# Bounding the weights of a two-layer kernel: products of upper halves on TensorE in place of sums of absolute values on ScalarE

## The chip, the cores and the metric

One core of a Trainium2 chip runs the whole program. The metric is the device time of one execution in microseconds; the median of the runs is compared. Engines are named as the profile names them: PE is TensorE, DVE VectorE, ACT ScalarE, POOL GpSimd, and SP the queue that issues the transfers.

## The reference

Attention over pooled keys and values, then a two-layer block with a softmax-weighted linear unit and a layer norm. Inputs of the attention are float32, the weights `w_in` (512 x 1024), `w_out` (1024 x 512) and the gain come in as 64-bit numbers.

```python
# attention: B, H, S, D = 8, 8, 576, 64; keys and values pooled by 8
k_p = k.reshape(B, H, Sp, pool, D).mean(axis=3)
v_p = v.reshape(B, H, Sp, pool, D).mean(axis=3)
scores = scale * np.matmul(q, k_p.transpose(0, 1, 3, 2))
attn = softmax(scores)                      # over the 72 pooled keys
attn_out = np.matmul(attn, v_p)
# block: x is 4608 x 512
h = x @ w_in                                # 4608 x 1024
e = np.exp(h - h.max(-1)); sm = e / e.sum(-1)
solu = h * sm
ln = (solu - mean) / np.sqrt(var + 1e-06) * g_ln
return (ln @ w_out).astype(np.float32)      # 4608 x 512
```

## The kernel before

The 4608 rows of x are worked off in 36 tiles of 128. Per tile, `scores` (16 small matmuls), a softmax on DVE and ACT (`s_max`, `s_sub`, `s_exp`, `e_sum`, `e_rec`, `e_mul`, split by `e_hi` and `e_lo` into two f16 parts, turned by a DMA transpose `e_T`), `av` (16 matmuls of 128 columns into the PSUM tile xp), `x_hi` and `x_lo` (xT in two f16 parts), `mm1` (24 matmuls of 512 columns into hp, in three parts), `h_max` to `z_var` on DVE, ACT and POOL, two transposes `z_T`, `mm2` (24 matmuls into op) and the store. Everything that TensorE multiplies is split into a high and a low f16 part, so that three passes give nearly float32.

Before tile 0 the two weights must be brought into such pairs. Each weight is loaded as 64-bit words in four chunks of 128 partitions x 1024. For a chunk `w_exp` (ACT, the prelude that puts the upper word into float32 shape, into a tile u), `w_shift` (DVE), `w_tail` (DVE, which puts the lower bits in) make float32 of it. In between `w_abs` (ACT) sums the absolute values along the row into a column of bnd. `w_rmax` (DVE) takes the maximum over the four columns, `w_par` (PE, a matmul that spreads it over partitions), `w_all` (DVE) and `wi_scale` or `wo_scale` (DVE, small instructions ending in sw or sg) turn it into a power of two as scale. Then `w_hi` (ACT) writes the high part, and the low part comes for wi from `w_res` on PE (two pairs of a float32 matmul and a "minus" matmul into a PSUM tile res of tag h) and `w_lo` on ACT, for wo from `w_lo` on DVE. Tile 0 uses all high parts first (part 0 of `mm1` and `mm2`), the low parts last (part 2).

Each engine works in the order in which its instructions are issued. That order is a table, ORDER, of numbers of operations: a planner outside the kernel made it, and `op` only records each operation with its dependencies. Tags of buffers matter in three places: the scores use a single PSUM tile (tag s), which `e_mul` frees; hp and res share two (tag h); op has one (tag o). The names in the rows: u_wi and u_wo are the words after `w_exp`, wo and wir (for wi) and wor (for wo) hold the raw words, amx_q and amx_v the maxima of q and v, qm is the q of a mixed tile, vr and v the parts of the pooled v.

Of the kernel before, what the change touches and what calls it, by code (L numbers as in the profile page):

```python
# [9 lines left out]
BF16 = mybir.dt.bfloat16  # L10
# [150 lines left out]
def kernel(  # L161
# [363 lines left out]
    def w_shift(nm, c):  # L525
# [3 lines left out]
        )  # L529


    def w_abs(nm, c):
        st = wst[nm]
        if "bnd" not in st:
            st["bnd"] = const.tile([P, 4], F32, name=f"bnd_{nm}")
# [898 lines left out]
```

## Time and profile before

| | us |
|---|---|
| median of 3 runs | 481.98 |
| lowest and highest | 481.43, 486.75 |
| the profiled execution | 480.16 |
| its span on the core | 478.3 |
| PE busy in it | 443.8 (93%) |
| DVE, ACT, POOL busy | 357.6, 349.5, 334.4 |

The span is what the instructions of the core take from the first to the last; the execution's own time is 1.9 us longer. The granted clock is 1.00 (of 2.4 GHz) over the whole span. A row of the order of time gives a start, a length, the engine, the line, the tile written and read, and in brackets how long the engine had been idle before it and what it waited for.

### The profile page before, as it was taken

How to read it: one execution, taken by the hardware profiler on the slowest of the kernel's cores; microseconds unless marked ns; L12 is line 12 of the kernel's file. 1: busy time of each engine (PE TensorE's matmuls, PEld its weight loads, DVE VectorE, ACT ScalarE, POOL GpSimd, SP SyncE). 2: the span in 40 equal slices, each digit the busy share in tenths (PEclk: the TensorE clock that was granted, in tenths of full speed). 3: DMA queues.
4: the chain of work that ended last, by engine and by line, in shares of the span. 5: the costliest groups of instructions: out<-in, count | busy, mean ns of one | idle time of the engine just before them, and what ended most of it. 6: DMA issues, size and time to landing. Idle time of an engine off the chain costs nothing.

```text
span 478.3 us, 9037 instructions
## 1 busy us (share of the span) xinstructions
PE 443.8 (93%) x3100; PEld 230.5 (48%) x3100; DVE 357.6 (75%) x865; ACT 349.5 (73%) x578; POOL 334.4 (70%) x466
## 2 busy tenths in 40 slices
PE   0177999999999999999999999999999999999996
PEld 0033544555454555555545554555555554554462
DVE  4989999589777976778667986887776989674520
ACT  1889999859877588766976788668866589567751
POOL 7145889768999678995897659985987448526440
PEclk9999999999999999999999999999999999999999
DMA  8999795899899879989878779887999387656341
GB/s 275 413 372 176 203 156 106 208 230 213 176 242 178 214 165 201 213 206 214 201 176 163 184 188 201 215 191 173 212 210 195 61 188 119 103 113 144 80 119 58
DMA packets 201389, 89.14 MB, mean 186 GB/s; under 512 B 177664, under 2 KB 186112, under 8 KB 200832
## 3 DMA queue, kind: packets, MB, share of 16 engines
q1 hardware_dynamic: 201344, 88.57, 80.1%
q8 instruction: 24, 0.39, 0.4%
q14 instruction: 21, 0.17, 0.1%
HBM read 36.70 MB, written 9.44 MB: 96 GB/s over the span
## 4 chain that ended last, share of the span: by engine, by line
PE 74%; DVE 8%; DMA 6%; ACT 4%; POOL 4%; issue 2%; SPq 0%; POOLq 0%; ACTq 0%; DVEq 0%
PE op L1008 33%; PE hp L876 32%; PE xp L844 6%; DMA qT<-q 3%; PE sc L754 3%; POOL z L943 1%; DMA qr<-in_q_dram 1%; ACT wo L651 1%; DMA zT<-z 1%; DVE amx_q L349 1%; DMA eT<-e 1%; DVE z L921 1%; DVE e L794 1%; DVE sc L779 1%; DVE mx L765 1%
## 5 line engine op out<-in xcount | busy, mean ns | idle before, releaser
L876 PE MATMUL hp<-wi,xT 128*128 128x512 f16 x864 | 196.2, 379 | 3.2 <-ACT xT L852 3.2
L1008 PE MATMUL op<-wo,zT 128*128 128x512 f16 (+1 forms) x888 | 197.3, 373 | 1.0 <-ACT osb L1016 0.6
L876 PEld LDWEIGHTS <-xT 128*128 128x128 f16 x864 | 82.6, 98 | 97.8 <-ACT xT L852 4.0
L1008 PEld LDWEIGHTS <-zT 128*128 128x128 f16 x888 | 84.7, 98 | 91.7 <-issue 1.0
L943 POOL TENSOR_TENSOR z<-z,z 128x512 f16<-128x512 f32 x71 | 82.0, 1170 | 37.9 <-ACT z L930 35.5
L886 DVE TENSOR_REDUCE m<-hp 128x1 f32<-128x1024 f32 x36 | 44.0, 1222 | 30.5 <-PE hp L876 30.2
L823 POOL TENSOR_TENSOR e<-e,e 128x512 f16<-128x512 f32 x36 | 42.0, 1166 | 21.6 <-ACT e L816 21.6
L330 POOL TENSOR_TENSOR vr<-vr 128x512 f32<-128x512 f32 (+3 forms) x48 | 48.6, 1015 | 12.1 <-DMA vr<-in_v_dram 11.6
L897 ACT ACTIVATE z<-hp,nb,Hb 128x1024 f32<-128x1024 f32 x32 | 38.4, 1199 | 23.7 <-DVE nb L889 20.1
L935 ACT ACTIVATE z<-z,sz 128x1024 f16<-128x1024 f32 x36 | 41.2, 1144 | 17.0 <-DVE z L921 17.0
L921 DVE SCALAR_TENSOR_TENSOR z<-hp,rs,z 128x1024 f32<-128x1024 f32 x36 | 46.1, 1280 | 3.2 <-ACT z L897 1.6
L330 POOL TENSOR_TENSOR kr<-kr 128x512 f32<-128x512 f32 (+3 forms) x48 | 41.8, 878 | 2.8 <-DMA kr<-in_k_dram 2.3
L765 DVE TENSOR_REDUCE mx<-sc 128x8 f32<-128x576 f32 x36 | 27.2, 754 | 21.0 <-PE sc L754 20.9
L930 ACT ACTIVATE z<-z,sz 128x1024 f32<-128x1024 f32 x36 | 41.2, 1145 | 0.7
L844 PEld LDWEIGHTS <-vb 128*128 128x128 f16 x640 | 35.3, 98 | 8.9 <-issue 0.8
L1016 ACT ACTIVATE osb<-op,f 128x512 f32<-128x512 f32 (+1 forms) x37 | 24.7, 668 | 18.9 <-PE op L1008 10.8
L844 PE MATMUL xp<-eT,vb 128*128 128x128 f16 (+1 forms) x640 | 38.2, 214 | 0.1
L956 ACT ACTIVATE junk<-z 128x1024 f16<-128x1024 f32 x36 | 37.7, 1047 | 0.4
L735 POOL TENSOR_TENSOR q<-qr,q 128x512 f16<-128x512 f32 x28 | 32.6, 1169 | 4.7 <-ACT q L725 4.7
L779 DVE TENSOR_REDUCE sc<-sc 128x8 f32<-128x576 f32 x36 | 27.4, 760 | 11.4 <-ACT sc L775 11.4
L852 ACT ACTIVATE xT<-xp 128x512 f16<-128x512 f32 x36 | 21.3, 592 | 17.5 <-PE xp L844 17.3
L856 DVE SCALAR_TENSOR_TENSOR xT<-xp,xT 128x512 f16<-128x512 f32 x36 | 24.6, 682 | 6.7 <-ACT xT L852 6.7
(230 smaller groups left out, 585.3 us busy)
## 6 DMA issues: line engine op xcount, KB each, us to landing
kr<-in_k_dram SPq DMA_DIRECT2D x16, 512.0 KB, 4.3
qr<-in_q_dram SPq DMA_DIRECT2D x16, 512.0 KB, 4.9
vr<-in_v_dram SPq DMA_DIRECT2D x16, 512.0 KB, 4.6
out_dram<-osb SPq DMA_DIRECT2D x31, 256.0 KB, 2.8
wor<-in_moe_w_out_dram SPq DMA_DIRECT2D x4, 1024.0 KB, 8.9
wo<-in_moe_w_in_dram SPq DMA_DIRECT2D x2, 1024.0 KB, 6.7
wir<-in_moe_w_in_dram SPq DMA_DIRECT2D x2, 1024.0 KB, 10.7
out_dram<-osb SPq DMA_DIRECT2D x10, 128.0 KB, 2.3
```

What stands on the lines that cost most here:

```text
L330: nc.gpsimd.tensor_tensor(out=dst, in0=src[:, :, :n], in1=src[:, :, n : 2 * n], op=ALU.add)
L823: nc.gpsimd.tensor_tensor(out=m[:, 1], in0=e_pair(i)[:, :, :P], in1=m[:, 0], op=ALU.subtract)
L844: nc.tensor.matmul(xp[:, c, lo:hi], lhsT=vb[b % 2][:, x, c].rearrange("p j d -> p (j d)"), rhs=eT[:, e, lo:hi], start=(n == 0), stop=(n == 3),
L876: nc.tensor.matmul(hp[:, f], lhsT=xT[:, xt, c], rhs=wi[:, wt, c, f * 512 : (f + 1) * 512], start=(part == 0 and n == 0), stop=(part == 2 a ...
L886: nc.vector.tensor_reduce(out=small(i, "m"), in_=tl[i]["hp"], axis=AX.XY, op=ALU.max)
L897: nc.scalar.activation(z, t["hp"], AF.Exp, bias=t["nb"], scale=hsc(i, 0), accum_out=small(i, "se"))
L921: nc.vector.scalar_tensor_tensor(out=t["z"], in0=t["hp"], scalar=t["rs"], in1=t["z"], op0=ALU.mult, op1=ALU.mult, accum_out=small(i, "sz"),)
L930: nc.scalar.activation(t["zf"], t["zf"], AF.Identity, bias=t["sz"], scale=-float(DFF))
L935: nc.scalar.activation(t["z16"][:, 0], t["zf"], AF.Identity, bias=t["sz"], scale=-float(DFF))
L943: eng.tensor_tensor(out=t["z16"][:, 1, fs], in0=t["zf"][:, fs], in1=t["z16"][:, 0, fs], op=ALU.subtract)
L956: nc.scalar.activation(junk, t["zf"], AF.Square, scale=DFF**-0.5, accum_out=small(i, "V"))
L1008: nc.tensor.matmul(op_, lhsT=zT[:, zt, c], rhs=wo[:, wt, c, cols(hf)], start=(part == 0 and n == 0), stop=(part == 2 and n == len(todo) - 1),)
```

## The change

`w_abs` is replaced by `w_gram`: the upper 16 bits of each shifted word are read as bfloat16 (every second 16-bit word of u), and each block of 128 columns is multiplied with itself on PE, all 8 blocks of the 4 chunks of a weight summed into one 128 x 128 PSUM tile of tag o. Its diagonal holds sums of squares, and `w_rmax` takes the maximum of it per partition. `w_bound` halves the exponent instead of only masking it. The operations are recorded for PE instead of ACT, `w_rmax` reads the PSUM tile, and ORDER is new throughout. The diff without most of ORDER:

```diff
-    2, 1, 0, 3, 4, 12, 11, 56, 5, 6, 57, 53, 54, 7, 58, 50, 55, 8, 180, 51, 52, 13, 181, 65, 9, 75,
...
+    2206, 2208, 2207, 2262, 2263, 2209, 2210, 2162, 2211, 2212, 2163, 2164, 2165, 2166,
 )
...
-    def w_abs(nm, c):
+    def w_gram(nm, c):
         st = wst[nm]
-        if "bnd" not in st:
-            st["bnd"] = const.tile([P, 4], F32, name=f"bnd_{nm}")
-        g = p1.tile([P, DFF], BF16, tag="junk", name=f"ab_{nm}{c}")
-        src = w_word(nm, c, 1).bitcast(F32) if (nm, c) in LOW else st["u", c]
-        nc.scalar.activation(g, src, AF.Abs, accum_out=st["bnd"][:, c : c + 1])
+        if "gram" not in st:
+            st["gram"] = ps_o.tile([P, DM], F32, tag="o", name=f"gram_{nm}")[:, :P]
+        if (nm, c) in LOW:
+            top = w_word(nm, c, 1).bitcast(F32).unsqueeze(2).bitcast(BF16)[:, :, 1]
+        else:
+            top = st["u", c].bitcast(BF16).rearrange("p (f t) -> p f t", t=2)[:, :, 1]
+        for n in range(DFF // P):
+            x = top[:, n * P : (n + 1) * P]
+            nc.tensor.matmul(
+                st["gram"], lhsT=x, rhs=x, start=(c == 0 and n == 0),
+                stop=(c == 3 and n == DFF // P - 1),
+            )
...
-        nc.vector.tensor_reduce(out=st["g1"], in_=st["bnd"], axis=AX.X, op=ALU.max)
+        nc.vector.tensor_reduce(out=st["g1"], in_=st["gram"], axis=AX.X, op=ALU.max)
...
-        nc.vector.tensor_scalar(out=gm, in0=gm, scalar1=2.0**-80, scalar2=None, op0=ALU.max)
-        exp_bits(gm, gm)
+        nc.vector.tensor_scalar(
+            out=gm.bitcast(I32), in0=gm.bitcast(I32), scalar1=1, scalar2=EXPMASK,
+            op0=ALU.logical_shift_right, op1=ALU.bitwise_and,
+        )
+        nc.vector.tensor_scalar(
+            out=gm, in0=gm, scalar1=2.0**64, scalar2=2.0**-60, op0=ALU.mult, op1=ALU.max
+        )
...
-            n = op("dve", 0.69, t, w_shift, nm, c, u=[u], after=last_u, w=[("u2", nm, c)])
-            bd.append(op("act", 1.15, t + 0.8, w_abs, nm, c, r=[("u2", nm, c)], u=[u],
-                         w=[("junk", nm, c)]))
+            op("dve", 0.69, t, w_shift, nm, c, u=[u], after=last_u, w=[("u2", nm, c)])
+            bd = [op("pe", 0.8, t + 0.8, w_gram, nm, c, r=[("u2", nm, c)], u=[u],
+                     w=[("o", "gram", nm)], after=bd)]
...
-        op("dve", 0.16, t_sum, w_rmax, nm, after=bd, w=[("g1", nm)])
+        op("dve", 0.16, t_sum, w_rmax, nm, r=[("o", "gram", nm)], w=[("g1", nm)])
```

LOW is empty, so only the second branch of `w_gram` is used. What the new ORDER does is shown at three places. The first is DVE at the last chunk of wi: the shift of u_wi3, the tail that writes wir3, the maximum g1_wi and the scale pwi. Before:

```order
L527 TENSOR_SCALAR u_wi3_233<-u_wi3_233 128x1024
L548 SCALAR_TENSOR_TENSOR wir3_158<-wir3_158,u_wi3_233 128x1024
L605 TENSOR_REDUCE g1_g_241<-g_sb_107 128x1
L556 TENSOR_REDUCE g1_wi_247<-bnd_wi_221 128x1
L560 TENSOR_REDUCE gm_wi_252<-g_wi_249 128x1
```

The same stretch of DVE now:

```order
L527 TENSOR_SCALAR u_wi3_250<-u_wi3_250 128x1024
L742 SCALAR_TENSOR_TENSOR q16_1_238<-qr0_141,sq('b', 0)_191,q16_1_238 128x8x64
L555 SCALAR_TENSOR_TENSOR wir3_157<-wir3_157,u_wi3_250 128x1024
L563 TENSOR_REDUCE g1_wi_270<-gram_wi_205 128x1
L440 TENSOR_SCALAR ct('b', 0)_274<-pq('b', 0)_190,pk0_177 128x1
L567 TENSOR_REDUCE gm_wi_278<-g_wi_276 128x1
```

The low part of q for tile 1 (q16_1, `q_lo(1)`) came four DVE instructions after the first shift before and now stands between the last shift and its tail; the maximum over the gain (g1_g, `g_max`) has gone from here to the start, and ct (`s_scale`) has come in behind the maximum.

The second place is DVE at the softmax of tile 1 and x of tile 0: e1 is written by `e_mul(1)`, v2_0 and vr by the two `v_lo` of batch 0, mx2 by `s_max(2)`, u_wo1 and u_wo2 by `w_shift`. Before:

```order
L785 TENSOR_SCALAR sc1_326<-sc1_326 128x2x4
L349 TENSOR_REDUCE amx_q_102<-qm0_306 128x1
L789 RECIPROCAL r1_381<-sc1_326 128x8
L527 TENSOR_SCALAR u_wo1_369<-u_wo1_369 128x1024
L794 TENSOR_TENSOR e1_390<-sc1_326,r1_381 128x576
L371 TENSOR_REDUCE pq('m', 0)_394<-gq('m', 0)_386 128x1
L468 SCALAR_TENSOR_TENSOR v2_0_379<-vp_0_92,sv0_344,v2_0_379 128x256
L468 SCALAR_TENSOR_TENSOR vr_97<-vp_0_92,sv0_344,vr_97 32x128
L376 TENSOR_SCALAR pq('m', 0)_394<-pq('m', 0)_394 128x1
L765 TENSOR_REDUCE mx2_428<-sc2_399 128x8
L201 TENSOR_SCALAR pq('m', 0)_394<-pq('m', 0)_394 128x1
L527 TENSOR_SCALAR u_wo2_392<-u_wo2_392 128x1024
```

Now, in two pieces of DVE's order with eight rows left out between them:

```order
L797 TENSOR_SCALAR sc1_350<-sc1_350 128x2x4
L468 SCALAR_TENSOR_TENSOR v2_0_408<-vp_0_92,sv0_383,v2_0_408 128x256
L801 RECIPROCAL r1_423<-sc1_350 128x8
L468 SCALAR_TENSOR_TENSOR vr_97<-vp_0_92,sv0_383,vr_97 32x128
L806 TENSOR_TENSOR e1_428<-sc1_350,r1_423 128x576
L371 TENSOR_REDUCE pq('m', 0)_434<-gq('m', 0)_410 128x1
...
L868 SCALAR_TENSOR_TENSOR xT0_504<-xp0_476,xT0_504 128x512
L527 TENSOR_SCALAR u_wo2_468<-u_wo2_468 128x1024
L806 TENSOR_TENSOR e2_528<-sc2_439,r2_508 128x576
L349 TENSOR_REDUCE amx_q_102<-qr1_420 128x1 x2
```

Both `v_lo` have moved ahead of `e_mul(1)`, and the shift of wo's chunk 2 (u_wo2) has moved behind `x_lo(0)` (xT0), ahead of the two maxima over q of batch 1 (amx_q from qr1).

The third place is the queue of SP, where the transfers are issued: wor2 is chunk 2 of wo, qT2 the transposed q of tile 2, eT0 the transposed softmax of tile 0. Before:

```order
L504 DMA wor1_243<-in_moe_w_out_dram 128x2x1024
L314 DMA qm0_306<-in_q_dram 64x8x64 x2
L504 DMA wor2_316<-in_moe_w_out_dram 128x2x1024
L742 DMA_TRANSPOSE qT2_321<-q16_2_279 128x8x128
L300 DMA kr1_2_351<-in_k_dram 64x512
L834 DMA_TRANSPOSE eT0_383<-e16_0_98 128x10x128
```

Now:

```order
L504 DMA wor1_268<-in_moe_w_out_dram 128x2x1024
L314 DMA qm0_327<-in_q_dram 64x8x64 x2
L300 DMA kr1_2_338<-in_k_dram 64x512
L754 DMA_TRANSPOSE qT2_343<-q16_2_272 128x8x128
L504 DMA wor2_348<-in_moe_w_out_dram 128x2x1024
L846 DMA_TRANSPOSE eT0_401<-e16_0_98 128x10x128
```

The load of wo's chunk 2 has gone from ahead of q's transpose for tile 2 to behind it. On PE the products of wo's chunk 1 stand right ahead of part 0 of `mm1(0)`, those of chunk 2 behind its part 1, and those of chunk 3 between `av(1)` and `mm1(1)`.

## Rows read from the trace of the kernel before

**Rows 1.** The page's first part: busy time, share of the span and instructions of each engine.

```profile
PE 443.8 (93%) x3100; PEld 230.5 (48%) x3100; DVE 357.6 (75%) x865; ACT 349.5 (73%) x578; POOL 334.4 (70%) x466
```

**Rows 2.** Busy time by stretches: from and to, length, then PE, weight loads, DVE, ACT and POOL busy with their instructions, the granted clock, the share of the DMA engines and what they moved.

```profile
33.00:45.00 12.00, 8.83 (x58) 4.31 (x55) 11.78 (x24) 10.93 (x21) 4.43 (x6) 1.00 0.92 227
45.00:57.00 12.00, 11.09 (x88) 6.15 (x89) 11.93 (x30) 11.12 (x23) 11.18 (x13) 1.00 1.03 221
57.00:70.00 13.00, 13.00 (x79) 6.52 (x77) 12.79 (x30) 13.00 (x19) 9.62 (x10) 1.00 0.87 142
...
200.00:300.00 100.00, 100.00 (x690) 51.74 (x689) 76.19 (x189) 75.41 (x127) 77.85 (x107) 1.00 0.85 192
```

**Rows 3.** What PE waited for over the whole span (total, times, longest); the last row is the longest of the four between 60 and 460 us.

```profile
PE g_wi L358 <- DVE g_wi L556: 10.6, 1, 10.6
...
PE hp L876 <- ACT xT L852: 3.2, 4, 2.0
...
PE op L1008 <- ACT osb L1016: 0.6, 2, 0.3
```

**Rows 4.** The sums of absolute values by their line (lengths in ns: shortest, median, longest), and matmuls in order of time: 16 scores early, and two "minus" matmuls of the residue, one behind the other.

```profile
L538 ACT ACTIVATE ab_wi<-u_wi x4: 1038/1048/1081, 16.9 to 22.7; 128x1024 bf16<-128x1024 f32 x4
...
25.29 1.14 PE L754 MATMUL sc<-kT,qT 128*128 128x72 f16 x16 [0.88 <-DMA qT<-q]
...
35.11 0.38 PE L672 MATMUL res_wi<-wi,minus 128*128 128x512 f16 x1
...
36.22 0.38 PE L672 MATMUL res_wi<-wi,minus 128*128 128x512 f16 x1
```

**Rows 5.** In order of time, around the last chunk of wi: the low part of q for tile 1, the prelude on ACT, the shift, the tail, the maximum and the reciprocal on DVE.

```profile
15.11 0.73 DVE L730 SCALAR_TENSOR_TENSOR q<-qr,sq('b', 0)_176,q 128x512 f16<-128x512 f32 x1
...
20.43 1.22 ACT L515 ACTIVATE u_wi<-wir 128x1024 f32<-128x1024 f32 x1 [0.24 <-DMA wir<-in_moe_w_in_dram]
...
21.68 0.69 DVE L527 TENSOR_SCALAR u_wi<-u_wi 128x1024 int32<-128x1024 int32 x1
22.40 1.23 DVE L548 SCALAR_TENSOR_TENSOR wir<-wir,u_wi 128x1024 int32<-128x1024 int32 x1
...
23.90 0.16 DVE L556 TENSOR_REDUCE g_wi<-bnd_wi 128x1 bf16<-128x4 f32 x1 [0.19 <-ACT ab_wi L538]
...
25.33 0.16 DVE L580 RECIPROCAL sw_wi<-pwi 128x1 f32<-128x1 f32 x1
```

**Rows 6.** In order of time, from the scores' maximum of tile 0 to the first matmul of hp.

```profile
26.46 0.76 DVE L765 TENSOR_REDUCE mx<-sc 128x8 f32<-128x576 f32 x1 [0.80 <-PE sc L754]
...
27.14 1.19 DVE L730 SCALAR_TENSOR_TENSOR q<-qr,sq('b', 0)_176,q 128x512 f16<-128x512 f32 x1
...
29.10 0.71 ACT L775 ACTIVATE sc<-sc,ct('b', 0)_212 128x576 f32<-128x576 f32 x1 [1.71 <-DVE sc L768]
...
38.19 0.75 DVE L794 TENSOR_TENSOR e<-sc,r 128x576 f32<-128x576 f32 x1
...
39.09 0.68 PE L754 MATMUL sc<-kT,qT 128*128 128x72 f16 x16 [1.20 <-DVE e L794]
...
39.99 1.23 DVE L468 SCALAR_TENSOR_TENSOR vr<-vp,sv,vr 32x128 f16<-32x128 f32 x1
...
41.91 1.06 PE L844 MATMUL xp<-eT,vb 128*128 128x128 f16 x16
42.04 0.68 DVE L527 TENSOR_SCALAR u_wo<-u_wo 128x1024 int32<-128x1024 int32 x1
...
44.30 0.59 ACT L852 ACTIVATE xT<-xp 128x512 f16<-128x512 f32 x1
...
44.95 3.63 PE L876 MATMUL hp<-wi,xT 128*128 128x512 f16 x16 [1.98 <-ACT xT L852]
```

**Rows 7.** In order of time, from the second maximum over q of batch 1 to the first matmuls of op; the row of wo in eight pieces is from the chain of work that ended last, the last three rows are PE's alone.

```profile
47.78 1.21 DVE L349 TENSOR_REDUCE amx_q<-qr 128x1 bf16<-128x1024 f32 x1
...
49.11 1.89 PE L876 MATMUL hp<-wi,xT 128*128 128x512 f16 x8
...
52.81 1.90 PE L876 MATMUL hp<-wi,xT 128*128 128x512 f16 x8 [0.91 <-ACT xT L852]
...
55.45 1.28 DVE L921 SCALAR_TENSOR_TENSOR z<-hp,rs,z 128x1024 f32<-128x1024 f32 x1
...
56.78 1.15 ACT L935 ACTIVATE z<-z,sz 128x1024 f16<-128x1024 f32 x1 [0.80 <-DVE z L921]
...
59.45 5.25 ACT wo L651 x8
...
64.13 1.06 PE L844 MATMUL xp<-eT,vb 128*128 128x128 f16 x16
65.02 3.62 PE L1008 MATMUL op<-wo,zT 128*128 128x512 f16 x16
68.47 1.89 PE L876 MATMUL hp<-wi,xT 128*128 128x512 f16 x8
```

**Rows 8.** The load of wo's chunk 2: its issue from 27.5 us on with its size and the time from issue to landing; then SP's hold by the transpose of q for tile 2, and the prelude of that chunk on ACT.

```profile
wor<-in_moe_w_out_dram SPq DMA_DIRECT2D x1, 1024.0 KB, 9.6
...
29.09 4.74 SPq L742 DMA_TRANSPOSE qT<-q  x1
...
39.37 1.12 ACT L515 ACTIVATE u_wo<-wor 128x1024 f32<-128x1024 f32 x1
```

More of the change, by code (lines that the diff above doesn't have):

```diff
@@ L1179, in weight @@
             if (nm, c) in LOW:
-                n = op("pool", 1.3, t, w_low, nm, c, r=[("w", nm, c)], w=[("wl", nm, c)], u=[rk])
+                op("pool", 1.3, t, w_low, nm, c, r=[("w", nm, c)], w=[("wl", nm, c)], u=[rk])
                 op("dve", 1.22, t + 2.0, w_tail, nm, c, r=[("wl", nm, c)], u=[u, rk],
                    w=[("wf", nm, c)], after=last_u)
-                bd.append(op("act", 1.15, t + 0.8, w_abs, nm, c, r=[("wf", nm, c)], u=[rk],
-                             w=[("junk", nm, c)]))
+                bd = [op("pe", 0.8, t + 3.2, w_gram, nm, c, r=[("wf", nm, c)], u=[rk],
+                         w=[("o", "gram", nm)], after=bd)]
                 continue
-            n = op("dve", 0.69, t, w_shift, nm, c, u=[u], after=last_u, w=[("u2", nm, c)])
-            bd.append(op("act", 1.15, t + 0.8, w_abs, nm, c, r=[("u2", nm, c)], u=[u],
-                         w=[("junk", nm, c)]))
+            op("dve", 0.69, t, w_shift, nm, c, u=[u], after=last_u, w=[("u2", nm, c)])
+            bd = [op("pe", 0.8, t + 0.8, w_gram, nm, c, r=[("u2", nm, c)], u=[u],
+                     w=[("o", "gram", nm)], after=bd)]
             op("dve", 1.22, t + 2.0, w_tail, nm, c, r=[("u2", nm, c)], u=[u, rk],
                w=[("wf", nm, c)])
-        op("dve", 0.16, t_sum, w_rmax, nm, after=bd, w=[("g1", nm)])
+        op("dve", 0.16, t_sum, w_rmax, nm, r=[("o", "gram", nm)], w=[("g1", nm)])
         op("pe", 0.4, t_sum + 0.2, w_par, nm, r=[("g1", nm)], w=[("x", "g", nm)])
```

260 rows, old and new, of the table ORDER are left out of this document.

## The prediction

> **What bounds the kernel now.** I read the page first, then the busy time by stretches, then the waits of PE, then the order of time from 14 to 66 us. PE is busy 443.8 of 478.3 us [rows 1]. By stretches it is idle almost only early: from 57 to 70 us it works 13.00 of 13, from 200 to 300 us 100.00 of 100 [rows 2]. Its waits say the same: 10.6 us for the bound of the first weights, 3.2 us for x transposed, and between 60 and 460 us nothing above 0.6 us [rows 3]. So after tile 0 has begun the kernel is a stream of matmuls, and its end moves one for one with two instants: the first matmul of hp for tile 0 (44.95 us, after an idle wait of 1.98 us for xT on ACT) and the first matmul of op for tile 0 (65.02 us) [rows 6, 7].
>
> What sets those instants is not PE. From 33 to 57 us DVE works 11.78 + 11.93 of 24 us and ACT 10.93 + 11.12 [rows 2]: DVE has 0.3 us to spare in 24, ACT 1.9 us. DVE's work is not reduced by the change. That is the heart of the forecast: ACT is relieved in a stage that DVE paces as well.
>
> **The change part by part.**
>
> *Removed from ACT*: eight sums of absolute values, 1.05 us each (1048 ns) [rows 4]: 8 x 1.05 = 8.4 us, four of them before 24 us and four between 40 and 54 us. Only one is waited for: the maximum over the bounds started 0.19 us after DVE was free [rows 5].
>
> *Added to PE*: 64 pairs of weight load and matmul, 128 columns each. The nearest rows are the 16 pairs of xp, which start at 64.13 us and give way at 65.02 [rows 7]: 0.89 / 16 = 56 ns a pair, 0.45 us for the eight of one chunk. Early in the program PE is slower: 16 scores take 1.14 us at 25.29 and 0.68 at 39.09 [rows 4, 6], though the granted clock is shown as 1.00 in both stretches; so I put 0.9 us on a chunk of wi. The operand is read every second 16-bit word, which no matmul of before does. The nearest row is the residue's matmul, which reads every second 32-bit word: from one "minus" matmul to the next is 36.22 - 35.11 = 1.11 us [rows 4], less 3.45 / 16 = 0.22 us for the f16 matmul in it (the 16 of op begin at 65.02 and the next hp at 68.47) [rows 7], leaving 0.89 us for 512 columns or 0.22 for 128; eight would be 1.8 us. The ends are 0.45 and 1.8; I take 0.45, since most of the 0.89 may be f32 itself. The Trainium skill's page "TensorE: Matmul & The Clock Gate", section "Back-to-back issue gap", gives about 81 ns for a sustained pair of 128 columns; by it a chunk would be an estimated 0.65 us, and the xp rows here disagree with it.
>
> Where these lie: the four chunks of wi and wo's chunk 0 stand where PE waits anyway (10.6 us before g_wi [rows 3]). Chunk 1 stands between av(0) and mm1(0,0), in the 1.98 us wait, chunk 3 between av(1) and mm1(1,0), where PE waited 0.91 us [rows 6, 7]. Chunk 2 stands after mm1(0,1), and the wait behind it (term 3 below) covers it. So PE's new work costs 0 to the end; without cover, 3 x 0.45 = 1.35 us.
>
> *Term 1, the scale of wi*. The last chunk of wi lands at 20.43 us and sets its prelude on ACT; the shift follows at 21.68 [rows 5]. That is a transfer, so it stays. Before, w_tail(wi,3) and g_max came next and the maximum at 23.90. Now q_lo(1) (0.73 us at 15.11 [rows 5]) stands between shift and tail: 21.65 + 0.70 + 0.73 + 1.2 = 24.3 us. The eight products of chunk 3 are done by 22.35 + 0.9 + 0.2 = 23.45, so the new wait ends earlier than DVE comes to it; at 1.8 us a chunk, at 24.35, it would add 0.1. The reduction reads 128 instead of 4 columns; I add 0.1, and s_scale, which has moved in behind it, fits into DVE's wait for PE's spreading. The reciprocal that gives sw_wi followed the maximum by 25.33 - 23.90 = 1.43 us [rows 5]; it comes at 24.3 + 0.1 + 1.43 = 25.8: **+0.5**.
>
> *Term 2, from there to x of tile 0*. DVE's idle wait of 0.80 us for the scores before s_max(0) [rows 6] goes, since q_lo(2) now stands in it, so that s_sub(0) ends about 0.6 us earlier and ACT starts s_exp(0) at 28.5 instead of 29.10: -0.6. It is given back at tile 1. Both v_lo (the second alone 1.23 us) now stand ahead of e_mul(1), which was at 38.19, and they wait for v_hi on ACT, which comes after s_exp(1): the sum is s_sub(1) at 34.5, s_exp(1) 35.35 to 36.05, v_hi until 37.45, v_lo until 39.7, e_mul(1) until 40.5. Behind e_mul(1) are queued on PE scores(2), whose PSUM it frees (PE waited 1.20 us for it before as well, until 39.09), the residue of wi's chunk 2 and av(0) [rows 6]. From scores(2) to av(0) is 41.91 - 39.09 = 2.8 us, av(0) 0.9: av(0) ends at 44.2, x_hi(0) starts at 44.3. On ACT I come to the same: the queue from s_exp(0) to x_hi(0) is 14.8 us of work, without w_abs(wo,0) but with h_bat and the long e_hi(1,0), and about 1 us of waits for DVE; 28.5 + 15.8 = 44.3. Before it was 44.30 [rows 6]. mm1(0,0) stays at 44.95: **0**. Here is where ACT's 8.4 us go: it waits for DVE instead.
>
> The same q_lo took 0.73 us once and 1.19 us once [rows 5, 6], the latter beside POOL's sums over v. The Trainium skill's "SBUF — State Buffer", section "SBUF: two separate sides", has DVE with two SBUF inputs and GpSimd exclude each other on a shared port pair, which these rows fit; by it the first v_lo, whose POOL neighbour v_put(0,0) now comes last, would be an estimated 0.4 us shorter, and e_mul(1) as much earlier.
>
> *Term 3, the shift of wo's chunk 2* (0.68 us at 42.04 [rows 6]) has moved behind x_lo(0), ahead of both maxima over q of batch 1. The second of them (47.78, 1.21 us) is waited for by a_par and then mm1(0,2) at 49.11 [rows 7]: less one small instruction (0.1) that is: **+0.55**. This wait covers wo's chunk 2 on PE.
>
> *Term 4, to mm2(0,0)*: a 128-wide maximum over wo's products (+0.1) and one a_scale (+0.15) now stand before z_mul(0); with term 3 that is z_mul(0) at 55.45 + 0.8 = 56.3. Behind it hangs what did before: z_hi(0) (which waited 0.80 us for it), z_cen(0), and the eight w_hi of wo, 5.25 us [rows 7], then mm2(0,0). ACT has no w_abs any more, but it waits for z_mul(0). **+0.3**, so +0.85 for the start of op, rounded to +0.9.
>
> *The rest*. PE's new order from tile 4 on is the old one with single pieces exchanged, and every path from scores to av, av to hp and hp to op holds much the same matmuls; the last 17 pieces are the same. I put 0 on it, with 0.5 either way, about the longest wait there now. The transfers: g_ln's load ahead of q, kr's pieces in another order (pooled k about 1 us later), q_T(0) 1.5 us later; k and qT(0) have that to spare, the latter since its issue is held behind the weights in any case. wo's chunk 2 goes behind q_T(2): see rival A.
>
> Sum: of +0.5 (term 1) and -0.6 nothing is left at 44.95 (term 2), then 0.55 + 0.3 = 0.85, about 0.9 us. The profiled execution took 480.16 us (span 478.3); it becomes 481.1. The median shown, 481.98, lies 1.8 us higher; on its scale the forecast is **482.9 us**.
>
> **The rivals.** *A, slower: wo's chunk 2 comes late.* SP issues q_T(2) before it now. Before, that load, issued ahead of it, landed 9.6 us after its issue, and q_T(2) held SP for 4.74 us from 29.09 [rows 8]. If q_T(2) holds SP until 33.8 as before, the load lands at 33.8 + 9.6 = 43.4. On ACT w_exp(wo,2), before at 39.37, would wait for it, with s_exp(2) and x_hi(0) queued behind: 43.4 + 1.1 + 0.3 + 0.7 + 0.6 = 46.1 against 44.30, +1.8, and eT(0), behind the load on the same queue, could make it +3: 484.6 to 485.8 with terms 3 and 4. It decides if the load lands after 40.5. Against it: q_T(0) and q_T(1) ended their issue about when an earlier transfer landed, and with the 1 MB load out of the way q_T(2) should find room at 30, the load then landing at about 38.7. *B, faster: ACT was the pace.* If the waits for DVE that I counted (v_lo behind v_hi, ACT behind s_sub) shrink, the gain is bounded by DVE's idle time, 0.8 us before s_max(0) and 0.3 from 33 to 57 us, and by 1.19 - 0.73 = 0.46 us for each of two slow instructions (q_lo, v_lo) [rows 5, 6]: at most 2.0 us, which gives 480.0. *C, the products are slow*: at 1.8 us a chunk, chunks 1 to 3 outlast their waits by 0 + 1.25 (1.8 less term 3) + 0.9 (1.8 less 0.91): 485.0. *D, the change does nothing*: the relief falls wholly into waits and the terms cancel: 482.0.
>
> **How the numbers follow.** Forecast (with D inside its width, 481.5 to 484.3) 0.6; A 0.15; B 0.15; C 0.1. The range leaves out half of B's far end and the worst of A: 480.4 to 485.5. One per cent, about what a measurement of this kernel can tell from no change, is 4.8 us: faster would need 477.2, beyond B's bound: 0.03. Slower needs 486.8, which A reaches only with a second late transfer: 0.07. The same: 0.90.
>
> **What would show it.** In the profile after: no w_abs on ACT, which is idle in 33 to 57 us for over 4 us; DVE still above 11.3 of 12; the products in bursts of about 0.45 us; sw_wi near 25.8; mm1(0,0) within 1 us of 44.95, mm2(0,0) near 65.9; PE full after that. It would be wrong if x_hi(0) came before 43 us (B) or w_exp(wo,2) waited for a transfer (A).

## The result, and the profile after

The changed kernel takes 485.12 us (median of 20 runs, 483.8 to 487.15), the kernel before 481.91 in the same set: ratio 1.0063 [1.0044, 1.0081], 3.0 us slower. That is inside one per cent and inside the forecast's range, but 2.2 us above the forecast itself. Runs that take over 1.5% longer than the fastest run of the same kernel are left out of all ratios, which are therefore not the quotients of the medians. The profiled execution took 484.96 us, its span 483.2.

The page's first part of the changed kernel answers to [rows 1]:

```profile
PE 450.2 (93%) x3164; PEld 235.0 (49%) x3164; DVE 361.3 (75%) x865; ACT 341.8 (71%) x562; POOL 332.0 (69%) x466
```

PE has 64 matmuls more, ACT 7.7 us less. The stretches of [rows 2] and two more, from 82 and from 106 us (same columns):

```profile
33.00:45.00 12.00, 9.40 (x73) 4.79 (x69) 11.40 (x22) 10.27 (x17) 5.19 (x7) 1.00 1.16 293
45.00:57.00 12.00, 11.31 (x102) 6.68 (x100) 11.95 (x29) 7.91 (x16) 9.05 (x11) 1.00 0.83 160
57.00:70.00 13.00, 13.00 (x85) 6.76 (x84) 12.79 (x33) 12.31 (x19) 10.61 (x10) 1.00 0.80 176
82.00:94.00 12.00, 10.60 (x91) 5.18 (x90) 9.13 (x24) 11.07 (x23) 8.18 (x11) 1.00 1.07 173
106.00:120.00 14.00, 12.97 (x88) 6.53 (x87) 12.40 (x32) 10.68 (x18) 10.30 (x12) 1.00 1.10 218
200.00:300.00 100.00, 99.67 (x695) 51.49 (x692) 76.38 (x191) 74.17 (x123) 78.19 (x105) 1.00 0.96 189
```

The two added stretches in the kernel before:

```profile
82.00:94.00 12.00, 11.47 (x86) 5.64 (x84) 7.71 (x20) 10.11 (x21) 8.92 (x13) 1.00 0.94 166
106.00:120.00 14.00, 14.00 (x104) 7.68 (x105) 13.50 (x34) 12.86 (x20) 12.54 (x18) 1.00 0.92 223
```

From 45 to 57 us ACT now idles 4.1 us and DVE is as full as before. PE is less full later: it misses 1.4 us between 82 and 94, where it missed 0.5 before, and 1.0 between 106 and 120, where it missed nothing. The order of time on PE (in brackets the idle time and what ended it) shows which waits these are:

```profile
83.08 0.68 PE L766 MATMUL sc<-kT,qT 128*64 128x72 f16 x31 [0.45 <-DMA kT<-k]
84.22 3.63 PE L1020 MATMUL op<-wo,zT 128*128 128x512 f16 x16 [0.46 <-DMA zT<-z]
88.02 1.90 PE L1020 MATMUL op<-wo,zT 128*128 128x512 f16 x8 [0.18 <-DMA zT<-z]
...
115.49 0.69 PE L766 MATMUL sc<-kT,qT 128*128 128x72 f16 x16 [1.03 <-DMA qT<-q]
```

The first part of the program, to be held against [rows 5 to 7]:

```profile
21.93 1.16 ACT L515 ACTIVATE u_wi<-wir 128x1024 f32<-128x1024 f32 x1 [0.75 <-DMA wir<-in_moe_w_in_dram]
...
23.87 1.03 PE L542 MATMUL gram_wi<-u_wi 128*128 128x128 bf16 x8 [1.37 <-DVE u_wi L527]
...
27.09 0.16 DVE L592 RECIPROCAL sw_wi<-pwi 128x1 f32<-128x1 f32 x1
...
40.54 0.76 DVE L806 TENSOR_TENSOR e<-sc,r 128x576 f32<-128x576 f32 x1
...
42.40 1.13 ACT L515 ACTIVATE u_wo<-wor 128x1024 f32<-128x1024 f32 x1
...
46.20 3.63 PE L888 MATMUL hp<-wi,xT 128*128 128x512 f16 x16 [0.41 <-ACT xT L864]
...
49.66 0.62 PE L542 MATMUL gram_wo<-u_wo 128*128 128x128 bf16 x8
...
50.79 1.89 PE L888 MATMUL hp<-wi,xT 128*128 128x512 f16 x8
...
57.17 1.28 DVE L933 SCALAR_TENSOR_TENSOR z<-hp,rs,z 128x1024 f32<-128x1024 f32 x1
...
66.66 3.62 PE L1020 MATMUL op<-wo,zT 128*128 128x512 f16 x16
```

Op of tile 0 begins 1.64 us later than in [rows 7]. That looked like half of the loss; the experiments say otherwise.

### The profile page after: what moved, and what is told of

The parts are those of the page before. It is cut to its first block, busy times and chain, and to the rows that moved or that the text cites. A ratio compares the mean times of both kernels' runs of the same rounds, so it can differ in the third digit from the quotient of the medians.

```text
span 483.2 us, 9140 instructions
## 1 busy us (share of the span) xinstructions
PE 450.2 (93%) x3164; PEld 235.0 (49%) x3164; DVE 361.3 (75%) x865; ACT 341.8 (71%) x562; POOL 332.0 (69%) x466
## 4 chain that ended last, share of the span: by engine, by line
PE 58%; POOL 12%; DVE 11%; DMA 11%; ACT 3%; issue 3%; SPq 2%; POOLq 0%; ACTq 0%
PE op L1020 29%; PE hp L888 23%; DMA qT<-q 5%; PE xp L856 4%; DMA zT<-z 3%; POOL kr L330 3%; PE sc L766 2%; POOL z L955 2%; DMA wo<-in_moe_w_in_dram 2%; POOL q L747 1%; POOL e L835 1%; POOL vr L330 1%; DVE mx L777 1%; DVE wor L555 1%; DMA kr<-in_k_dram 1%
```

## The experiments

The table divides each profiled execution at the first matmul of op for tile 0 (first column of numbers, us); the second is the span less that. Medians (of 12 runs, 5 in e5 and 6 in e6) and ratios are of the timed runs, each against before in its own set. The median of before is 481.91 us in the set of the changed kernel, 481.08 for e1 to e4, 482.31 for e5 to e8, 482.70 for e9 to e11 and 483.23 for e12; why it varies is told under the clock, further down.

| kernel | op begins | from there to the end | median | ratio [95%] |
|---|---|---|---|---|
| before | 65.02 | 413.3 | 481.91 | |
| before again (e11) | 66.68 | 412.8 | 483.04 | 1.0028 [0.9993, 1.0063] |
| changed | 66.66 | 416.5 | 485.12 | 1.0063 [1.0044, 1.0081] |
| e1 products, old order | 68.72 | 413.2 | 483.29 | 1.0036 [1.0015, 1.0057] |
| e2 sums, new order | 69.89 | 413.7 | 485.73 | 1.0083 [1.0057, 1.0109] |
| e3 gain behind q | 66.21 | 417.2 | 485.09 | 1.0069 [1.0044, 1.0094] |
| e4 new, then old | 66.69 | 412.9 | 481.43 | 0.9997 [0.9973, 1.0021] |
| e5 SP's order old | 67.52 | 431.8 | 501.31 | 1.0402 [1.0375, 1.0429] |
| e6 POOL's order old | 67.27 | 417.3 | 485.31 | 1.0068 [1.0049, 1.0088] |
| e7 new to tile 5 | 67.92 | 415.1 | 483.86 | 1.0038 [1.0024, 1.0051] |
| e8 old to tile 5 | 66.83 | 413.6 | 482.05 | 1.0000 [0.9984, 1.0016] |
| e9 short piece first | 67.23 | 417.2 | 484.95 | 1.0050 [1.0017, 1.0084] |
| e10 and q earlier | 66.61 | 416.1 | 484.77 | 1.0032 [0.9999, 1.0065] |
| e12 short stretch old | 67.16 | 415.0 | 482.89 | 1.0008 [0.9978, 1.0038] |

**Products and order apart (e1, e2).** The operations have the same numbers in both kernels, so that either table of order fits either code. In e1 the four products of wo, which the old table has on ACT, got places on PE.

```diff
 code: changed kernel
-ORDER = the changed kernel's
+ORDER = the kernel before's, on PE w_gram(wo,0..3) behind a_par(v,0,1), av(0), mm1(0,1), av(1)
```

> The products on TensorE, but in the table of the kernel before; only the four products of wo are put where PE waits or nearly so (behind the spreading of v's maximum, av(0), part 1 of hp for tile 0, av(1)). Theory 1 (the new order costs the 3 us, the products nothing): within 1 us of the kernel before, first matmul of hp within 0.5 us of 44.95. Theory 2 (the products on PE, or what hangs on them, cost it): 2 to 4 us slower, like the changed kernel.

```diff
 code: kernel before
-ORDER = the kernel before's
+ORDER = the changed kernel's
```

> The sums of absolute values stay on ScalarE, but the table is that of the changed kernel (each sum stands where the product of its chunk stood). Theory 1 (the new order costs it): 3 us slower than before or more, since ACT has also the eight sums of 1.05 us to do. Theory 2 (the products cost it): within 1 us of the kernel before.

Measured: 1.0036 and 1.0083. E2 bears out theory 1: with the sums still on ACT the new order costs 4 us. E1 meets neither theory: it is 1.7 us slower than before, and its first matmul of hp comes at 48.48 us. With the new order, products instead of sums bring op forward by 69.89 - 66.66 = 3.2 us, but the end by only 485.73 - 485.12 = 0.6: with op late, the part behind it takes 413.7 us, with op early 416.5. What PE no longer waits for ahead of op it waits for behind it. In e1 the part behind op is as short as before; its loss is in front, where q's transpose for tile 2, issued at 30.62 in the old order, landed 11.6 us later, and TensorE's clock fell behind the wait (0.50 from 43 to 46 us); all 12 of its runs have a mean granted clock of 0.992 to 0.996. First the wait on PE, then the stretches around it (the granted clock is the third figure from the end):

```profile
42.27 0.69 PE L766 MATMUL sc<-kT,qT 128*128 128x72 f16 x16 [2.55 <-DMA qT<-q]
```

```profile
39.00:42.00 3.00, 0.73 (x4) 0.10 (x1) 2.97 (x7) 2.96 (x6) 1.67 (x3) 1.00 1.08 105
42.00:45.00 3.00, 2.73 (x19) 1.45 (x20) 2.94 (x6) 1.10 (x3) 1.26 (x2) 0.64 1.09 273
```

**The gain's load (e3).**

```diff
 SP, DVE:
-load_g() ahead of load_q(0,0) ... g_max() at the start
+load_g() behind load_q(0,1) ... g_max() right ahead of w_rmax(wi)
```

> The changed kernel with two operations put back: the load of g_ln (4 KB in pieces of 4 bytes) is issued behind q's loads again, and the maximum over it stands right before the maximum over wi's products. Theory 1a (that load, ahead of q, delays q and all weights behind it): the last chunk of wi is ready for its prelude near 20.5 instead of 21.93 us, the first matmul of hp comes 1 to 1.3 us earlier, the time is 1 to 1.5 us below the changed kernel, a ratio near 1.004 to the kernel before. Rival 1b (the front is later for another reason: k's pieces in another order, SP issuing its loads slower): the last chunk stays at 21.5 to 22 and the time at that of the changed kernel.

Measured: 1.0069; nothing changes. The load of the gain ahead of q is not the cause.

**Where in the program (e4, e7, e8).**

```diff
+e4: new order up to and with mm2(0,0), the rest in the order of before
+e7: new order up to and with mm2(5,2), the rest in the order of before
+e8: new order to mm2(0,0), the order of before to mm2(5,2), then the new one
```

> The changed kernel's order up to the first part of op for tile 0 (all operations that stand before it in the table), then the order of the kernel before. Theory 1c (about half of the loss is in waits behind that point, for transposes between 82 and 116 us): the start of op stays near 66.7 us, the waits for kT, zT and qT between 82 and 116 us go from 2.1 us to under 1, and the time is 1 to 1.5 us below the changed kernel. Rival (those waits follow from the late start, whatever the order): the waits and the time stay as in the changed kernel.

> The changed kernel with the new order on all engines up to the last part of op for tile 5 (about 125 us), and the order of before from there. If the loss is made in the cluster of waits at 82 to 116 us it stays: 484 to 485.3 us. If it is made by the single waits later in the span it goes: 481.5 to 482.5 us. Of the 3.7 us that separate the changed kernel from the one with the old order behind tile 0, I expect 2.5 here, thus 484.

> The mirror of the kernel before it: new order up to the first matmul of op for tile 0, the order of before from there to the last part of op for tile 5 (about 125 us), and the new order again to the end. If the loss is made at 82 to 116 us it goes: 481.4 to 482.5 us. If it is made by single waits later it stays: 484 to 485.3 us. I expect 482.6: 1.2 us of later waits for zT, 0.2 to 0.4 us each.

Measured: 0.9997, 1.0038, 1.0000. E4 starts op where the changed kernel does (66.69), with the products and the new first part in it, and equals the median of before. So the first part costs nothing that this median shows, and the loss lies behind op; it is 3.7 us, more than the 1 to 1.5 that I expected of e4. E8 puts most of it between 67 and 125 us: with that stretch in the old order, the new order after it costs little (482.05 us, in another set, against 481.43 in e4). E7 keeps the stretch and has 0.38 of the 0.63%; the rest comes only where the new order follows as well. The waits of PE tell the same. Added up from its order of time, from op of tile 0 to 126 us and from there to 465 us, they are 2.8 and 1.4 us in the changed kernel, 1.2 and 0.3 in e4, 3.4 and 0.3 in e7, 0.6 and 0.8 in e8, and 0.9 and 0.9 in the kernel before.

**Which engine (e5, e6).** From mm2(0,0) on, one engine alone goes back to the order of before.

```diff
+e5: SP's order of before, to the end
+e6: POOL's order of before, to z_lo(8,0)
```

> The changed kernel, with one engine's order alone put back: behind the first matmul of op for tile 0, SP issues its transfers in the order of before; PE, ACT, DVE and POOL keep the new order throughout. The loss sits behind that matmul, in waits for transposed k, z and q. Theory Q (the queue: q's loads and stores ahead of kr's loads and of qT make these late): 481.5 to 482.5 us, ratio at most 1.002, no wait for qT at 115 us. Theory P (POOL writes the low parts of z and the pooled k later in the new order, so that the transfers are issued later whatever their order): 484.5 to 485.5 us, the waits for kT and zT at 83 to 88 us stay.

> The changed kernel, with one engine's order alone put back in one stretch: behind the first matmul of op for tile 0 and as far as the low part of z of tile 8, POOL works in the order of before; all other engines keep the new order. Theory P (POOL's order makes z and k late): 482 to 483 us, ratio at most 1.003, and no wait for kT or zT of over 0.2 us between 82 and 94 us. Theory Q (the queue): 484.5 to 485.5 us, with the wait of about 1 us for qT near 115 us.

Neither decides between the theories by its time. E5 takes 501.31 us: its queue and the other engines no longer fit together.

```profile
PE xp L856 <- DMA eT<-e: 10.8, 6, 4.9
```

That is PE waiting for e transposed, 10.8 us in six times, the longest 4.9 (at 377 us), only one of the six, of 0.70 us at 97 us, in the stretch in question. In that stretch e5 does say something: with SP's order of before PE no longer waits for qT near 115 us, while the waits for kT (0.29) and zT (0.45) near 84 us stay. E6 stays at 1.0068, but by other waits: the one for qT is gone here too, the one for zT near 84 us stays (0.45), and new ones have come, the longest for zT:

```profile
169.10 1.90 PE L1020 MATMUL op<-wo,zT 128*128 128x512 f16 x8 [1.20 <-DMA zT<-z]
```

So e6 doesn't clear POOL's order: one engine put back alone makes waits of its own.

**The collision (e9, e10, e12).** The lines that write the low part of pooled k, two instructions on DVE (shortest, median, longest in ns), first in the changed kernel, then in e8:

```profile
L422 DVE SCALAR_TENSOR_TENSOR k<-kp,sk,k x2: 743/1189/1635, 77.2 to 78.7; 128x320 f16<-128x320 f32 x2
```

```profile
L422 DVE SCALAR_TENSOR_TENSOR k<-kp,sk,k x2: 625/686/747, 77.4 to 78.0; 128x320 f16<-128x320 f32 x2
```

The first one takes 1.63 us in place of 0.75 or less, in the changed kernel as in e3, e5 and e7. Beside it run POOL's sums over v; behind it stand the transpose of k and, queued on SP, the first of z for tile 2. In e8 these are issued at 78.76 and 80.19, here at 79.52 and 80.95, and two of the three waits of PE between 83 and 88 us are for them, 0.9 us together; the third has another cause, since the second transpose of z is as early as in e8. E8's order of time:

```profile
78.76 1.33 SPq L427 DMA_TRANSPOSE kT<-k  x1
80.19 1.35 SPq L963 DMA_TRANSPOSE zT<-z  x1
```

The changed kernel's, with one of POOL's rows first:

```profile
76.88 0.87 POOL L330 TENSOR_TENSOR vp<-vr 32x128 f32<-32x128 f32 x2
...
79.52 1.33 SPq L427 DMA_TRANSPOSE kT<-k  x1
80.95 1.38 SPq L963 DMA_TRANSPOSE zT<-z  x1
...
107.45 1.93 SPq L754 DMA_TRANSPOSE qT<-q  x1
```

The last row is the transpose behind the wait of 1.03 us; two loads and a store stand ahead of it. It isn't issued late. In e4, which starts op at the same time, it is issued later:

```profile
108.24 1.23 SPq L754 DMA_TRANSPOSE qT<-q  x1
```

There it lands 5.7 us after its issue and PE waits 0.31 us; in the changed kernel it lands after 8.0 us. So the landing is late, and not the issue, on which my expectation of e10 puts it.

```diff
 POOL (e9, e10):
+pool_kv(1,vr,2,2)
 pool_kv(1,vr,0,0), pool_kv(1,vr,1,0), z_lo(1,1), n_f(0), z_lo(1,0), pool_kv(1,vr,1,1)
-pool_kv(1,vr,2,2)
 SP (e10, e12):
 e_T(6)
+q_T(8)
 load_kv(2,vr,0), o_store(3), load_kv(2,kr,1)
-q_T(8)
 all engines (e12):
-mm2(0,0) to scores(5) in the new order
+mm2(0,0) to scores(5) in the order of before
```

> The changed kernel with one operation moved on POOL: the last sum over v's short piece for batch 1 (32 x 128) goes back ahead of the low part of z of tile 1, into a time in which POOL waits 2.6 us for DVE; nothing else moves. Theory K: in the new order that sum runs beside DVE's low part of pooled k and stretches it from 0.74 to 1.63 us; transposed k is issued 0.9 us later, and both transposes of z of tile 2, queued behind it on SP, too, which makes the three waits of 0.45, 0.46 and 0.18 us of PE at 83 to 88 us. By it both low parts of k take 0.75 us or less, these waits fall below 0.3 us together and the time is about 1 us below that of the changed kernel: 484.1 us. Rival: the stretched instruction is covered, the waits come from DVE's and ACT's new order; then the waits stay near 1.1 us and the time at 485.1.

> The kernel before this one, and on SP the transpose of q for tile 8 moved from behind two loads and a store to right behind the transpose of e of tile 6. Theory: the wait of 1.03 us for qT at 115 us, which the new order on SP made by queueing that transpose behind them until 107.5 us, goes; together with the short piece this takes back all that the new order loses between 69 and 125 us: 482 to 483.2 us, ratio to before at most 1.003. Rival: q's transpose is then held by the transfers in flight and lands when it did, or the later loads of k and v make a new wait behind 115 us: 484 us or more.

> The changed kernel with two stretches put back: from the first matmul of op for tile 0 to the scores of tile 5 (67 to 84 us) every engine works in the order of before (a dozen places exchanged on POOL, thirty small ones on DVE, two pairs on ACT, none on PE), and on SP the transpose of q for tile 8 follows that of e of tile 6, as two runs back. All else is new. Theory of the collisions: what the new order loses between 69 and 96 us is that one of DVE's instructions with two inputs from SBUF (a low part of k, or, once the short piece of v was moved, a low part of wo) meets one of POOL's in SBUF and takes 1.63 us instead of 0.74; put back together, the low parts of k are at 0.75 us or less, those of wo at 0.84 or less, PE waits below 0.3 us for kT, zT and osb before 88 us, and with q's transpose moved the time is 481.8 to 482.8 us, ratio at most 1.002, as with the whole stretch to 125 us put back. Rival: the loss lies in the order from 84 to 125 us, where the new order stays: 484 us or more.

E9 moved the sum as meant and gained nothing measurable (1.0050). The low parts of k are fast, but now one of the low parts of wo, also on DVE, is slow: the last one, from 73.3 us on (first row k, second wo, third what POOL does then):

```profile
L422 DVE SCALAR_TENSOR_TENSOR k<-kp,sk,k x2: 539/653/767, 79.1 to 79.8; 128x320 f16<-128x320 f32 x2
...
L692 DVE SCALAR_TENSOR_TENSOR wo<-wor,sg_wo,wo x8: 740/832/1644, 65.2 to 73.3; 128x512 f16<-128x512 f32 x8
...
73.04 1.40 POOL L955 TENSOR_TENSOR z<-z,z 128x512 f16<-128x512 f32 x1 [2.16 <-ACT z L942]
```

POOL's low part of z lies beside it, and PE's wait comes earlier, for osb at 78.39 (0.57 us). My expectation had this wrong: the collision was not removed, it changed partner. Nor does the loss need it: in e6 the longer low part of k takes 1.02 us, none of wo over 0.89, and the ratio is 1.0068. E10 takes the wait for qT away as well (PE waits for zT 0.20 at 117.54 instead) and stands at 1.0032; its interval holds no change and the 1.0050 of e9, so what q's transpose is worth by itself stays open. E12 exchanges a dozen places on POOL, thirty small ones on DVE, two pairs on ACT and none on PE. Its ratio is 1.0008, but against a median of before of 483.23, the highest of all sets. By its own time, 482.89 us, it has 2.2 us back of the 3.7 that separate the changed kernel (485.12) from e4 (481.43). It is 1.9 us below e10, from which it differs in the stretch from 67 to 84 us alone, or 1.2 when each is held against the runs of before at full clock in its own set (see the clock below). (Its profiled run, 484.0, is 1.1 above its own median.) Neither low part is slow (the row for wo begins with the second of eight; the first takes 0.88):

```profile
L422 DVE SCALAR_TENSOR_TENSOR k<-kp,sk,k x2: 629/688/747, 77.5 to 78.1; 128x320 f16<-128x320 f32 x2
...
L692 DVE SCALAR_TENSOR_TENSOR wo<-wor,sg_wo,wo x7: 737/741/841, 66.2 to 72.7; 128x512 f16<-128x512 f32 x7
```

PE's waits up to 126 us are down to 0.9 us, from 2.5 in e10, and there is none for kT, zT or osb before 88 us. Behind 126 us they are 2.3 us, more than the changed kernel's 1.4, the longest of them

```profile
166.61 1.90 PE L1020 MATMUL op<-wo,zT 128*128 128x512 f16 x8 [0.73 <-DMA zT<-z]
```

and one of 0.64 us, for zT too, at 347 us. So the order from 67 to 84 us is worth between 1 and 2 us; how much of that is the collision isn't shown, since e12 puts back everything in that stretch.

The profile shows which instructions are stretched and what runs beside them; that the cause is the pair of engines, and not, say, the addresses, is inferred: no run here takes one of the partners away. The Trainium skill's "SBUF — State Buffer", section "SBUF: two separate sides", has it so: a DVE instruction with two inputs from SBUF and a POOL instruction that reads SBUF share a pair of ports, the first to start holds it for its whole length, and the other waits. The runs agree in this too that either can lose: where the low part of k is fast, in the kernel before, a sum of POOL beside it takes 0.71 us (at 75.65) and its like 0.46 (at 77.37). That one of them holds the ports for its whole length no row here shows.

**Before again (e11).** No edit.

> The kernel before, unchanged, profiled a second time. In the first profile the last chunk of wi reached ACT at 20.43 us, and op of tile 0 began at 65.02; in all the profiles with the changed kernel's first part these are 21.5 to 22.9 and 66.7 to 67.9, although the time of some of them equals that of before. Theory R (the landing of the first loads varies from execution to execution by about 1 us, and the first profile of before caught an early one; its 480.16 us lie 1.8 below the median): here the last chunk comes at 21.3 to 22.0, op at 66 to 67, and the profiled execution takes 481.5 to 482.5 us. Theory O (the first part of the changed kernel does take 1.6 us more and gives it back later): 20.4 and 65.0 again.

Measured: 483.04 us beside 482.70 for the same kernel. Its profile, the chunk first, then the matmuls of the residue and op:

```profile
21.35 1.22 ACT L515 ACTIVATE u_wi<-wir 128x1024 f32<-128x1024 f32 x1 [0.18 <-DMA wir<-in_moe_w_in_dram]
...
33.56 0.29 PE L358 MATMUL gv<-identb,amx_v 128*128 128x128 bf16 x1 [2.69 <-DVE amx_v L349]
...
36.47 0.63 PE L672 MATMUL res_wi<-wi,minus 128*128 128x512 f16 x1
...
38.60 0.63 PE L672 MATMUL res_wi<-wi,minus 128*128 128x512 f16 x1
...
66.68 3.62 PE L1008 MATMUL op<-wo,zT 128*128 128x512 f16 x16
```

```profile
33.00:36.00 3.00, 2.44 (x19) 1.68 (x20) 2.99 (x7) 3.00 (x5) 0.00 (x0) 0.50 1.11 344
36.00:39.00 3.00, 3.00 (x5) 1.14 (x4) 2.85 (x9) 2.79 (x7) 1.42 (x2) 0.50 1.17 226
```

So the kernel before starts op at 66.68 as well: the last chunk came 0.92 us later than in [rows 5], and behind an idle time of 2.69 us PE worked at 0.50 (1.2 GHz) from 33 to 39 us: from one "minus" matmul to the next 38.60 - 36.47 = 2.13 us, where [rows 4] have 1.11. Of the 1.66 us by which op comes later than in [rows 7], 0.92 are thus the landing; the rest arises between the reciprocal and the first matmul of hp (20.38 us against 19.62), the stretch with the lower clock. The profile that the forecast was made from caught an early landing. Its time doesn't tell that: this execution took 481.22 us, below the 481.5 that I expected at least, and 1.8 below the median of its own set as well.

## Why the prediction came out as it did

**The bound.** That PE is the stream and DVE, not ACT, paces 33 to 57 us held: DVE 11.40 and 11.95 of 12, ACT idle. ACT's 8.4 us went into waits, as said. That the end moves one for one with the start of op did not hold (e2 against the changed kernel: 3.2 us there, 0.6 at the end).

**The products.** 0.46 us a chunk from 33 us on (33.38 to the next matmul at 33.84, and 49.66 to 50.12) against 0.45; 1.03 for a chunk of wi against 0.9. So reading the operand at every second 16-bit word costs nothing that shows, and the prediction's two other prices, 0.65 and 1.8 us, did not come. Rival C is out, though 485.0 was its time.

**Term 1**, +0.5: from the prelude of the last chunk to the reciprocal are 27.09 - 21.93 = 5.16 us, in the two profiles of before 4.90 and 4.88. So +0.3. The rest of the way to 27.09 is the landing of the chunk, 20.43, 21.35 and 21.93 in three profiles, which the forecast took as fixed.

**Term 2**, nothing left at the first matmul of hp: from the reciprocal to it 19.11 us, 19.62 before; forecast 19.15. Right, by its way too: e_mul(1) gives it back, starting at 40.54. The estimate that the first v_lo would be 0.4 us shorter held as well: 0.48 us against 0.90.

**Terms 3 and 4**, +0.85: from the first matmul of hp to op 20.46 us against 20.07, in both profiles of before. So +0.4: term 3 is there (4.59 against 4.16 us to mm1(0,2)), of term 4's +0.3 nothing is left, since z_mul(0) comes 0.47 later and op 0.39. Terms 1 to 4 together came to little: from the prelude of wi's last chunk to op are 66.66 - 21.93 = 44.73 us against 65.02 - 20.43 = 44.59.

**The rest**, 0 with 0.5 either way: this step failed, by about 3 us. From op to the end are 416.5 us, against 413.3 and 412.8 in the two profiles of before. It looked at PE's order alone, in which from tile 0 to tile 5 one pair of operations is exchanged, and concluded from that to equal waits. The waits come from the engines that feed it, DVE, ACT, POOL and SP, whose orders differ in that stretch: e8, in which PE's order differs by that one pair, and e12, in which it doesn't differ at all, take 3.1 and 2.2 us off the changed kernel's time. What one engine contributes is open, and so is the part that only the order behind 125 us brings (e7); there PE's own order differs in some thirty places too.

**Right, in part by luck.** "The same" held because 3 us are less than one per cent. That 485.12 us lies inside the range is luck: the forecast's own width ended at 484.3, and the range went on to 485.5 for rivals A and C, neither of which came.

**Rivals.** A did not decide: the load of wo's chunk 2 was issued at 34.04 and landed 6.4 us later, SP being held for 3.20 instead of 4.74, and w_exp(wo,2) at 42.40 waited for no transfer. B did not come, and D's terms cancel only in e4.

**What was also missed:** the clock. Of the 95 runs of before that the ratios of e1 to e12 rest on, 65 have a mean granted clock under 0.998, with a median of 482.56 us; the other 30 have 480.82 (480.35 to 481.03 us in the four sets). With the products in the new first part (changed kernel, e3, e4, e6 to e10, e12) all runs have 0.998 or more; e5, with waits of up to 4.9 us later on, has 0.988 to 0.997. So a ratio to before compares, in part, clocks. Against the runs of before at 0.998 or more in the same set, e4 is 0.8 us slower, e8 1.1, e12 2.5, e7 2.9, e10 3.7 and e9 3.9; the changed kernel, whose set lists no clocks for before, is 4.3 us slower than all 30. The medians of before in these four sets, raised by the lower clock, lie 0.5 to 2.9 us higher and hide that. That e4's 0.8 is near the forecast's 0.9 says nothing for the forecast's terms: the profiles put their sum at 44.73 - 44.59 = 0.14 us.

No version here beats the kernel before; e4, the products with the old order behind tile 0, equals it.

## What to carry over

A new order that leaves the busiest engine's sequence as it was can still cost: compare the sequences of the engines that feed it, and look where a two-input DVE instruction and one of POOL will now stand side by side. Here a gain ahead of a full engine (3.2 us, e2 against the changed kernel) was nearly all lost to waits behind. Profile the kernel before twice before taking the instant of a landing as fixed. Compare each run's mean granted clock as well as the medians: two kernels at different clocks can have equal medians.

## What was new of the hardware

TensorE's clock fell to 1.2 GHz in the middle of a busy program, behind idle times of 2.55 us (e1), 2.69 us (e11) and 4.88 us (e5, at 377 us), and stayed at 2.4 behind the 1.98 us of [rows 6]. Early in the program the granted clock doesn't tell the speed: in the kernel before, two "minus" matmuls start at 28.20 and 30.34 us, 2.14 us apart as at 0.50 in e11, and the clock is shown as 1.00. A DVE instruction of 0.74 us took 1.62 to 1.64 us beside POOL in six profiles, the low part of k in four (changed kernel, e3, e5, e7) and that of wo in two (e9, e10); the longer low part of k took 1.26 us in e2, 1.02 in e6, and 0.77 or less in all others.
